# One fused block on one core: the first keys by two queues, and the masks of some attention groups added by VectorE

## The chip, the cores and the metric

The kernel runs on one core of a Trainium2 chip. The metric is the device time of one execution in microseconds, the median of three runs. Engines are named as in the profile: PE is TensorE, DVE is VectorE, ACT is ScalarE, POOL is GpSimd, SP is SyncE. ACTq and SPq are the queues through which ScalarE and SyncE issue transfers (DMA).

## What is computed

Four batches of 576 tokens pass through three parts in a row: masked attention with 8 heads of 64, a gated feed-forward part with a product over the tokens, and a part with a sine and a cosine of projected phases and two more products over the tokens.

```python
scores = scale * np.matmul(q, k.transpose(0, 1, 3, 2))
mask_local = (rel >= 0) & (rel < 32)
mask_strided = (rel >= 0) & (pos[None, :] % 32 == pos[:, None] % 32)
scores = np.where(masks, scores, -1e9)            # heads 0-3 local, 4-7 strided
attn = softmax(scores); x = attn @ v              # heads side by side: 512 columns
h = np.maximum(x @ w_in, 0.0); u, v = halves of h
v_s = einsum('ts,bsd->btd', w_spatial, normalised v) + b_spatial
x = (u * v_s) @ w_out
theta = x @ w_theta; zr, zi = x * cos(theta), x * sin(theta)
y = w_tok_r applied to zr + w_tok_i applied to zi (over the tokens)
u = x + y; out = u + np.maximum(u @ w_ch, 0.0)
```

## The kernel before, in words

All matrix weights and activations are split into a high and a low float16 part, and each product is made of three TensorE products (`PASS`). The stages of a batch, by the names of the PSUM tiles, are `v`, then `u` and `sp` (the gated part), `x` (`w_out`), `th` (the phases), `y` (the tokens) and `c` (the last product). The loop at the end of the kernel runs them batch after batch, and the `v` products of the next batch stand ahead of the `y` products of this one.

The phase stage makes one tile `th` for each of four column blocks (`z_chunk`, line 953). ScalarE copies it to whole turns in a tile `ta`, VectorE subtracts these from the phase in PSUM (the first VectorE step on `ta`, which lets go of the PSUM tile), ScalarE takes the sines, VectorE multiplies by `x2f`, and high and low parts go to `vn` and by transposing transfers to `zf`. There are three such PSUM tiles (`pm`, line 202), shared by all stages; a fourth product tile waits until one of them is read out.

Weights come as raw 64-bit words. ScalarE, VectorE and GpSimd turn them into high and low parts while the first batch runs (`stage` and `from_f64`, lines 226 and 233; `tok_part`, line 306). `raw` tiles are the buffers `x2f`, `zf` and `xT`; the 32-bit value is `wx`; `win`, `wtok` and so on are the finished parts. GpSimd makes most low parts.

Attention of batches 0 to 2 is in float32, by nine groups of blocks (`groups`, line 423): groups 0 to 3 are four local blocks of 96 columns of keys each for head pair 0 or 1, group 4 the two last local blocks, groups 5 to 8 strided blocks of 64 columns. So a group is 384 columns wide, but group 4 has 192 and group 8 has 256. Group 6 also holds two blocks at the end of the sequence that are only 36 columns wide.

For each group `gr_scores` (line 504) makes the scores in PSUM and adds the mask there by one more TensorE product, or two, with the identity in bfloat16 (`identb`) and the mask repeated over the blocks. `gr_shift` (line 533) has VectorE take the row maxima from PSUM and write the scores minus maximum to `sm`. Then come the exponential (`gr_exp`), the transposes to `pT` (`gr_turn`), the product with the values and the division (`gr_pv`), and the transposes to `xT` (`gr_out`).

`attention0` (line 606) is batch 0. Nothing else runs beside it, and its instructions stay in program order on each engine. At its start SyncE loads query and keys of head pair 0 for the first four blocks, then ScalarE's queue loads the whole of pair 1, and a small exponential makes ScalarE load its table. `load_qk` (line 429) issues one transfer for the queries and two for the two heads' keys. Before it, `WARM` dummy products of the identity with itself run on TensorE (line 1077). `attention1` (line 661) makes batches 1 and 2 beside the stages of the batch before, a step at a time, each step due at a time in the table `ATT_AT`. Outside `attention0` a scheduler settles the order on each engine, with priority for the stages over attention. Batch 3 goes another way (`attention`, line 747), whose mask comes by a transfer and a cast on GpSimd (`load_mask16`, line 499). GpSimd casts it ahead of the low parts of `win`.

Of the kernel before, what the change touches and what calls it, by code (L numbers as in the profile page):

```python
# [17 lines left out]
AF = mybir.ActivationFunctionType  # L18
ALU = mybir.AluOpType
# [31 lines left out]
E_YLO = 'gggggggg'  # L51
E_YHI = 'vaavvaav'
E_ZLO = 'vvvvvvvv'
WARM = 6
ATT_AT = (None, (2.7, 3.9), (79.0, 5.4), (169.9, 4.6))
CONV_SP = (20.0, 9.9, 1.9)
CONV_OUT = (37.0, 12.0, 5.0)
# [8 lines left out]
def kernel(  # L66
# [52 lines left out]
    nc = Engines  # L119
    B, DM, S = out.shape  # L120
    P = 128
# [40 lines left out]
    halfpi = const.tile([P, 1], F32, name="halfpi")  # L162
# [30 lines left out]
    x2f = const.tile([P, NC, S], F32, name="x2f")  # L193
# [228 lines left out]
    QB, CB = 64, 54  # L422
# [3 lines left out]
               (False, [(3, i) for i in range(6)]), (False, [(3, i) for i in range(6, 10)])]  # L426
    NG = len(groups)

    def load_qk(b, hp, q, k, c0, c1, by=None):
        by = by or nc.sync  # L430
        local = hp < 2
        src = kzl[b, hp] if local else kzs[b, hp - 2]
        k0, k1 = (c0 + STRIDE if c0 else 0, c1 + STRIDE) if local else (c0, c1)
        by.dma_start(q[:, c0:c1], qp[b, hp][:, c0:c1])
        for j in range(2):
            h = slice(64 * j, 64 * j + 64)
            by.dma_start(k[h, k0:k1], src[h, j, k0:k1])

    def load_vl(b, hp, v):
        src = vl_d[b, hp].rearrange("p n j d -> p n (j d)")  # L440
# [60 lines left out]
        nc.sync.dma_start(mf, mask_d)  # L501
        nc.gpsimd.tensor_copy(mask, mf)

    def gr_scores(g, q, k, sc):

        local, blocks = groups[g]
        w = 96 if local else QB
        n = len(blocks)
        if local and blocks[0][1] == 0:
            runs = [(0, 1, mask64[:, 1]), (1, n, mask64[:, 0])]  # L510
        else:
            runs = [(0, n, mask64[:, 0] if local else mask54)]
        first = groups[g][0]

        def masks():
            for r0, r1, m in runs:
                nc.tensor.matmul(sc[:, r0 * w:r1 * w].rearrange("p (n c) -> p n c", c=w), identb,
                                 m.unsqueeze(1).broadcast_to([P, r1 - r0, w]), start=(not first and r0 == 0),
                                 stop=(first and r1 == n))

        if not first:
            masks()
        for i, (hp, blk) in enumerate(blocks):
            o = (QB if local else CB) * blk
            m, c = min(QB, S - o), w if local else min(w, S - o)
            for j in range(2):
                h = slice(64 * j, 64 * j + 64)
                nc.tensor.matmul(sc[64 * j:64 * j + m, i * w:i * w + c], q[hp][h, o:o + m], k[hp][h, o:o + c],
                                 start=(first and i == 0), stop=(not first and i == n - 1))
        if first:  # L530
            masks()

    def gr_shift(g, sc, sm, st):
        local, blocks = groups[g]
        n, w = len(blocks), 96 if local else QB
        mx = st[:, 0, 0:n]
        sv = sc[:, 0:n * w].rearrange("p (n c) -> p n c", c=w)
        nc.vector.tensor_reduce(out=mx, in_=sv, op=ALU.max, axis=mybir.AxisListType.X)
        nc.vector.tensor_tensor(sm[:, 0:n * w].rearrange("p (n c) -> p n c", c=w), sv,
                                mx.unsqueeze(2).broadcast_to([P, n, w]), ALU.subtract)  # L540
# [65 lines left out]
    def attention0(aside):  # L606
# [6 lines left out]
        q, k = [t[:, 0] for t in qk], [t[:, 1] for t in qk]  # L613
        v = [vf[:, i * 9 * VW:(i + 1) * 9 * VW].rearrange("p (n d) -> p n d", n=9) for i in range(2)]
        v23 = vf[:, 18 * VW:30 * VW].rearrange("p (h n d) -> p h n d", h=2, n=6)
        v += [v23[:, i] for i in range(2)]
        load_qk(0, 0, q[0], k[0], 0, 4 * QB)
        load_qk(0, 1, q[1], k[1], 0, S, nc.scalar)
        nc.scalar.activation(x2f[:, 0, 0:1], halfpi, AF.Exp)
        make_masks()  # L620
        load_qk(0, 0, q[0], k[0], 4 * QB, S)
        load_vl(0, 0, v[0])
# [8 lines left out]
        for s in range(NG + 3):  # L631
            mid, end = aside.get(s, ((), ()))
            if s < NG:
# [6 lines left out]
                sm, pT = t[:, 0, 0:384], t[:, 1, 0:512].rearrange("p (n k) -> p n k", n=4)  # L640
                st = att_p.tile([P, 2, 6], F32, tag="st", name="st", bufs=4)
# [3 lines left out]
            if s >= 3:  # L645
                banks, sm, pT, st = un.pop(s - 3)
# [14 lines left out]
    def attention1(b):  # L661
        q, k, v = {}, {}, {}
# [19 lines left out]
        for s in range(NG + 3):  # L682
            if s < NG:
                sm = att_p.tile([P, 384], F32, tag="sm", name="sm", bufs=2)
                pT = att_p.tile([P, 4, P], F32, tag="pT", name="pT32", bufs=2)
                st = att_p.tile([P, 2, 6], F32, tag="st", name="st", bufs=4)
                un[s] = (sm, pT, st)
            if s >= 3:
                gr_out(b, s - 3, xs.pop(s - 3), pa("sc"))
            if 2 <= s < NG + 2:  # L690
                sm, pT, st = un.pop(s - 2)
                pv = pa("av")[:, 0:3 * VW].rearrange("p (i n) -> p i n", i=3)
                gr_pv(s - 2, v, pT, pv, st, pT)
                xs[s - 2] = pT
            if s < NG:
                sm, pT, st = un[s]
                sc = pa("sc")
                gr_scores(s, q, k, sc)
                gr_shift(s, sc, sm, st)
                gr_exp(s, sm)  # L700
            if s in loads:
                f, hp = loads[s]
                f(hp)
                if s == 4:
                    load_a(3)
            if 1 <= s <= NG:
                sm, pT, st = un[s - 1]
                gr_turn(s - 1, sm, pa4("av"), pT)
            yield
# [485 lines left out]
```

## Time and profile before

| | |
|---|---|
| median of 3 runs | 505.43 us (505.38, 505.43, 506.62) |
| the profiled execution | 506.96 us, its span 505.1 us |
| TensorE busy | 485.1 us of the span |
| VectorE, ScalarE, GpSimd busy | 284.8, 267.8, 92.9 us |
| granted TensorE clock, mean over the span | 0.996 |
| transfers | 52.72 MB, mean 104 GB/s |

Times within the span are counted from its start. Busy time of an engine is the time in which it works on an instruction. In the timeline a row is one instruction, or a run of like ones with their count, with the start and the time it took; what stands in brackets is the idle time of the engine before it and what ended that. The operands are written as output, arrow, inputs, with the names of the tiles. All operations are recorded by one helper, so all have the line L103.

### The profile page before, as it was taken

The numbers are of one execution on the slowest core, as the hardware profiler recorded it, in microseconds if no ns is written. First come the engines' busy times: TensorE is split into PE (matmuls) and PEld (weight loads), VectorE is DVE, ScalarE is ACT, GpSimd is POOL, SyncE is SP. The second block draws the span as 40 slices with busy tenths as digits, with TensorE's granted clock in tenths as the row PEclk, the third lists the DMA queues.
The fourth block names the chain that finished last, engine by engine and source line by source line (L and its number), as shares of the span: only waits on it lengthen the run. The fifth ranks groups of instructions, "written<-read, shape, count | busy, mean of one in ns | idle before, by whom it ended". The sixth has DMA issues, their size and how long they took to land. (4 is left out here: it accounts for less than half of the span.)

```text
span 505.1 us, 10834 instructions
## 1 busy us (share of the span) xinstructions
PE 485.1 (96%) x4460; PEld 364.4 (72%) x4460; DVE 284.8 (56%) x607; ACT 267.8 (53%) x475; POOL 92.9 (18%) x91
## 2 busy tenths in 40 slices
PE   7889989998999999999999989999999999999996
PEld 5655757776567777888758867777657777777774
DVE  3765986555699343473499578772587121227412
ACT  2657788587994233345672757754862022149202
POOL 2042147225124400021003210021005200210220
PEclk9999999999899999999999999999999999999999
DMA  6868748377691024221080156230160020003402
GB/s 177 279 203 234 260 151 270 103 185 225 188 223 49 1 66 150 72 80 27 1 185 4 31 128 195 47 60 5 38 151 1 1 95 1 0 2 80 111 1 93
DMA packets 71788, 52.72 MB, mean 104 GB/s; under 512 B 50552, under 2 KB 59960, under 8 KB 71738
## 3 DMA queue, kind: packets, MB, share of 16 engines
q1 hardware_dynamic: 71434, 51.42, 36.5%
q8 instruction: 35, 0.57, 0.5%
q10 hardware_dynamic: 304, 0.61, 0.4%
q14 instruction: 15, 0.12, 0.1%
HBM read 35.36 MB, written 4.72 MB: 79 GB/s over the span
## 5 line engine op out<-in xcount | busy, mean ns | idle before, releaser
L103 PE MATMUL y<-wtok,zf 128*128 128x288 f16 x864 | 107.2, 286 | 1.0 <-DMA zf<-vn 1.0
L103 PEld LDWEIGHTS <-zf 128*128 128x128 f16 x864 | 84.1, 98 | 23.5 <-DMA zf<-vn 1.3
L103 PE MATMUL sp<-wsp,vn 128*128 128x288 f16 x384 | 52.2, 286 | 1.6 <-ACT vn L103 1.3
L103 PE MATMUL c<-x2h,wch 128*128 128x288 f16 x384 | 49.3, 286 | 2.3 <-ACT o L103 2.3
L103 PE MATMUL th<-x2h,wth 128*128 128x288 f16 x384 | 49.6, 291 | 2.0 <-DVE ta L103 2.0
L103 PE MATMUL x<-zf,wout 128*128 128x288 f16 x384 | 49.9, 286 | 0.0
L103 PE MATMUL u<-xT,win 128*128 128x288 f16 x384 | 49.7, 286 | 0.0
L103 PE MATMUL v<-win,xT 128*128 128x512 f16 (+1 forms) x240 | 48.4, 380 | 0.8 <-DVE xT L103 0.6
L103 PEld LDWEIGHTS <-vn 128*128 128x128 f16 x416 | 39.7, 98 | 12.1 <-ACT vn L103 1.4
L103 POOL TENSOR_TENSOR x2h<-x2f,x2h 128x576 f16<-128x576 f32 x20 | 25.5, 1279 | 119.1 <-ACT x2h L103 47.2
L103 PEld LDWEIGHTS <-wth 128*128 128x128 f16 x384 | 38.1, 100 | 12.5 <-issue 2.2
L103 PEld LDWEIGHTS <-wch 128*128 128x128 f16 x384 | 37.3, 98 | 11.8 <-issue 2.7
L103 PEld LDWEIGHTS <-win 128*128 128x128 f16 x384 | 37.3, 98 | 9.2
L103 PEld LDWEIGHTS <-wout 128*128 128x128 f16 x384 | 36.7, 98 | 9.6
L103 PEld LDWEIGHTS <-xT 128*128 128x128 f16 (+1 forms) x240 | 21.0, 100 | 25.2 <-issue 2.2
L103 ACT ACTIVATE x2h<-x2f 128x576 f16<-128x576 f32 (+1 forms) x28 | 20.9, 746 | 28.9 <-DVE x2f L103 28.4
L103 DVE SCALAR_TENSOR_TENSOR x2f<-y,x2f 128x576 f32<-128x576 f32 x16 | 12.0, 753 | 30.6 <-PE y L103 30.5
L103 DVE TENSOR_TENSOR u<-u,sp 128x576 f32<-128x576 f32 x16 | 12.0, 752 | 28.2 <-PE sp L103 28.2
L103 ACT ACTIVATE o<-c 128x576 f32<-128x576 f32 (+1 forms) x17 | 10.4, 616 | 32.1 <-PE c L103 31.8
L103 DVE TENSOR_TENSOR ta<-ta,x2f 128x1152 f32<-128x1152 f32 x16 | 21.5, 1354 | 9.8 <-ACT ta L103 9.8
L103 POOL TENSOR_TENSOR zf<-u,zf 128x576 f16<-128x576 f32 x8 | 10.7, 1340 | 86.0 <-ACT zf L103 86.0
L103 DVE TENSOR_TENSOR vn<-ta,vn 128x1152 f16<-128x1152 f32 x16 | 21.5, 1355 | 5.6 <-ACT vn L103 5.6
(140 smaller groups left out, 738.2 us busy)
## 6 DMA issues: line engine op xcount, KB each, us to landing
out_dram<-o SPq DMA_DIRECT2D x15, 288.0 KB
kt<-in_qp_dram SPq DMA_DIRECT2D x8, 288.0 KB
qs<-in_qd_dram SPq DMA_DIRECT2D x8, 288.0 KB
x2f<-in_w_in_dram SPq DMA_DIRECT2D x2, 1024.0 KB
zf<-in_w_in_dram SPq DMA_DIRECT2D x2, 1024.0 KB
xT<-in_w_ch_dram SPq DMA_DIRECT2D x2, 1024.0 KB
kt<-in_kzl_dram SPq DMA_DIRECT2D x8, 152.0 KB
ks<-in_kl_dram SPq DMA_DIRECT2D x4, 304.0 KB
```

Source lines behind the costliest of these rows:

```text
L103: ins = f(*args, **kwargs)
```

## The change

`WARM` is 7 in place of 6. `load_qk` takes a second queue for the second head's keys; the first load of all uses SyncE and ScalarE. The small exponential, and with it the table load, now stands ahead of ScalarE's three transfers of pair 1. `gr_scores` can leave the mask out and then hands it on; `gr_shift` then adds it on VectorE while it copies the scores to `sm`, and takes maximum and difference from there. `attention1` does so for batch 2, and for batch 1 from group 4 on, but never for group 6.

```diff
@@
-WARM = 6
+WARM = 7
@@
-    def load_qk(b, hp, q, k, c0, c1, by=None):
+    def load_qk(b, hp, q, k, c0, c1, by=None, by1=None):
@@
         for j in range(2):
             h = slice(64 * j, 64 * j + 64)
-            by.dma_start(k[h, k0:k1], src[h, j, k0:k1])
+            ((by1 if j else None) or by).dma_start(k[h, k0:k1], src[h, j, k0:k1])
@@
-    def gr_scores(g, q, k, sc):
+    def gr_scores(g, q, k, sc, add=True):
@@
-        if not first:
+        if not add:
+            first = True
+        elif not first:
             masks()
@@
                 nc.tensor.matmul(sc[64 * j:64 * j + m, i * w:i * w + c], q[hp][h, o:o + m], k[hp][h, o:o + c],
-                                 start=(first and i == 0), stop=(not first and i == n - 1))
-        if first:
+                                 start=(first and i == 0), stop=(not (first and add) and i == n - 1))
+        if first and add:
             masks()
-
-    def gr_shift(g, sc, sm, st):
+        return [] if add else runs
+
+    def gr_shift(g, sc, sm, st, runs=()):
+
@@
         sv = sc[:, 0:n * w].rearrange("p (n c) -> p n c", c=w)
+        for r0, r1, m in runs:
+            to = sm[:, r0 * w:r1 * w].rearrange("p (n c) -> p n c", c=w)
+            nc.vector.tensor_tensor(to, sv[:, r0:r1], m.unsqueeze(1).broadcast_to([P, r1 - r0, w]), ALU.add)
+        if runs:
+            sv = sm[:, 0:n * w].rearrange("p (n c) -> p n c", c=w)
         nc.vector.tensor_reduce(out=mx, in_=sv, op=ALU.max, axis=mybir.AxisListType.X)
@@
-        load_qk(0, 0, q[0], k[0], 0, 4 * QB)
+        load_qk(0, 0, q[0], k[0], 0, 4 * QB, None, nc.scalar)
+        nc.scalar.activation(x2f[:, 0, 0:1], halfpi, AF.Exp)
         load_qk(0, 1, q[1], k[1], 0, S, nc.scalar)
-        nc.scalar.activation(x2f[:, 0, 0:1], halfpi, AF.Exp)
@@
-                gr_scores(s, q, k, sc)
-                gr_shift(s, sc, sm, st)
+                gr_shift(s, sc, sm, st, gr_scores(s, q, k, sc, b == 1 and s < 4 or s == 6))
```

The scheduler's order on the engines moves with it. On ScalarE, at the start of the program (`kt_80` is head pair 0's tile, `kt_81` pair 1's; minus before, plus the change):

```order
+L103 DMA kt_80<-in_kzl_dram 64x288
+L103 ACT_TABLE_LOAD
+L103 ACTIVATE x2f<-halfpi 128x1
 L103 DMA kt_81<-in_qp_dram 128x576
 L103 DMA kt_81<-in_kzl_dram 64x608 x2
-L103 ACT_TABLE_LOAD
-L103 ACTIVATE x2f<-halfpi 128x1
```

One key transfer came to this queue, and pair 1's three moved behind the table load.

On ScalarE, in the phase stage of batch 0 (`xT_94` holds the last raw weight), before:

```order
L103 ACTIVATE xT_94<-xT_94 128x576
L103 ACTIVATE wtok<-wx 128x1152
L103 ACTIVATE wx<-xT_94 128x576
L103 ACTIVATE ta_1549<-th_1493 128x576
L103 ACTIVATE ta_1566<-th_1494 128x576
L103 ACTIVATE ta_1602<-th_1577 128x576
L103 ACTIVATE ta_1549<-ta_1549 128x576
L103 ACTIVATE wtok<-wx 128x576
L103 ACT_TABLE_LOAD
```

and now:

```order
L103 ACTIVATE xT_94<-xT_94 128x576
L103 ACTIVATE wx<-xT_94 128x576
L103 ACTIVATE ta_1550<-th_1494 128x576
L103 ACTIVATE ta_1567<-th_1495 128x576
L103 ACTIVATE wtok<-wx 128x1152
L103 ACTIVATE ta_1550<-ta_1550 128x576
L103 ACTIVATE ta_1567<-ta_1567 128x576
L103 ACT_TABLE_LOAD
```

The `wtok` write of 1152 columns went behind the first two phase copies, and the third phase copy went behind the table load and the first sines.

On VectorE at the same place, before:

```order
L103 SCALAR_TENSOR_TENSOR ta_1549<-th_1493,ta_1549 128x576
L103 SCALAR_TENSOR_TENSOR ta_1566<-th_1494,ta_1566 128x576
L103 SCALAR_TENSOR_TENSOR ta_1602<-th_1577,ta_1602 128x576
L103 TENSOR_REDUCE st<-sc 128x4
L103 TENSOR_TENSOR sm<-sc,st 128x384
L103 TENSOR_TENSOR ta_1549<-ta_1549,x2f 128x1152
L103 TENSOR_TENSOR vn<-ta_1549,vn 128x1152
L103 TENSOR_TENSOR ta_1566<-ta_1566,x2f 128x1152
L103 TENSOR_TENSOR ta_1602<-ta_1602,x2f 128x1152
L103 SCALAR_TENSOR_TENSOR ta_1638<-th_1613,ta_1638 128x576
```

and now:

```order
L103 SCALAR_TENSOR_TENSOR ta_1550<-th_1494,ta_1550 128x576
L103 SCALAR_TENSOR_TENSOR ta_1567<-th_1495,ta_1567 128x576
L103 TENSOR_TENSOR sm<-sc,mask_100 128x96
L103 TENSOR_TENSOR sm<-sc,mask_100 128x288
L103 TENSOR_REDUCE st<-sm 128x4
L103 TENSOR_TENSOR sm<-sm,st 128x384
L103 TENSOR_TENSOR ta_1550<-ta_1550,x2f 128x1152
L103 TENSOR_TENSOR ta_1567<-ta_1567,x2f 128x1152
L103 SCALAR_TENSOR_TENSOR ta_1603<-th_1578,ta_1603 128x576
L103 TENSOR_TENSOR vn<-ta_1550,vn 128x1152
L103 TENSOR_TENSOR vn<-ta_1567,vn 128x1152
L103 TENSOR_TENSOR ta_1603<-ta_1603,x2f 128x1152
```

The two mask additions of batch 2's group 0 came in, and the third step on `ta` moved behind two multiplications by `x2f`; the fourth stands directly behind the last row shown.

## Rows read from the trace of the kernel before

**Rows 1.** The page's part 1: busy time, share of the span, instructions

```profile
PE 485.1 (96%) x4460; PEld 364.4 (72%) x4460; DVE 284.8 (56%) x607; ACT 267.8 (53%) x475; POOL 92.9 (18%) x91
```

**Rows 2.** Waits of TensorE by releaser: total us, times, longest us

```profile
PE th L103 <- DVE ta L103: 2.0, 1, 2.0
```

**Rows 3.** Timeline of the start: start us, us, engine, operation [idle before <-releaser]

```profile
1.18 1.19 ACTq L103 DMA_DIRECT2D kt<-in_kzl_dram  x2
1.20 1.44 SPq L103 DMA_DIRECT2D kt<-in_kzl_dram  x2
...
1.36 2.93 PE L103 MATMUL av<-ident 128*128 128x128 f32 x12 [1.36 <-POOL ident masks.py:199]
...
5.04 5.30 SPq L103 DMA_DIRECT2D wtok<-in_vl_dram  x8
...
6.00 2.13 PE L103 MATMUL at<-kt 64*64 64x96 f32 x16 [1.71 <-DMA kt<-in_kzl_dram]
...
8.49 1.54 PE L103 MATMUL at<-kt 64*64 64x96 f32 x16
...
14.22 0.88 PE L103 MATMUL sc<-kt 64*64 64x96 f32 x16
```

**Rows 4.** Timeline from 26 us: mask transfer, GpSimd, first v products

```profile
27.25 0.36 SPq L103 DMA_DIRECT2D mf<-in_mask_dram  x1
...
30.81 0.85 POOL L103 CAST mask<-mf 128x512 bf16<-128x512 f32 x1 [26.68 <-DMA mf<-in_mask_dram]
...
31.62 2.26 POOL L103 TENSOR_TENSOR win<-x2h,win 128x512 f16<-128x512 f32 x2
...
33.94 0.38 PE L103 MATMUL v<-win,xT 128*128 128x512 f16 x1 [0.27 <-POOL win L103]
```

**Rows 5.** Timeline from 112 us: the phase stage of batch 0

```profile
121.25 0.73 ACT L103 ACTIVATE xT<-xT 128x576 f32<-128x576 f32 x1 [1.65 <-DMA xT<-in_w_ti_dram]
121.89 1.16 ACT L103 ACTIVATE wtok<-wx 128x1152 f16<-128x1152 f32 x1
...
122.94 0.72 ACT L103 ACTIVATE wx<-xT 128x576 int32<-128x576 uint8 x1
...
123.69 1.32 DVE L103 SCALAR_TENSOR_TENSOR wx<-xT,wx 128x576 int32<-128x576 int32 x1 [2.60 <-ACT wx L103]
124.94 1.41 DVE L103 SCALAR_TENSOR_TENSOR ta<-th,ta 128x576 f32<-128x576 f32 x2
...
125.73 4.66 PE L103 MATMUL th<-x2h,wth 128*128 128x288 f16 x24 [2.02 <-DVE ta L103]
...
130.22 11.94 PE L103 MATMUL v<-win,xT 128*128 128x512 f16 x60
...
137.35 0.75 DVE L103 SCALAR_TENSOR_TENSOR ta<-th,ta 128x576 f32<-128x576 f32 x1
```

**Rows 6.** Timeline of TensorE from 230 us: all phase products of batch 1

```profile
238.34 11.92 PE L103 MATMUL th<-x2h,wth 128*128 128x288 f16 x96
```

**Rows 7.** Windows: stretch, busy us (instructions) by engine, granted clock, DMA share, GB/s

```profile
7.00:8.00 1.00, 1.00 (x14) 0.83 (x10) 0.00 (x0) 0.00 (x0) 0.00 (x0) 1.00 0.63 161
16.00:17.00 1.00, 0.91 (x20) 0.66 (x19) 1.00 (x3) 0.95 (x3) 0.00 (x0) 1.00 1.12 323
127.00:128.00 1.00, 1.00 (x6) 0.62 (x5) 1.00 (x2) 0.98 (x3) 0.00 (x0) 0.50 0.98 401
```

**Rows 8.** Timeline from 145 us: one mask product and the product behind it

```profile
162.85 0.34 PE L103 MATMUL sc<-mask,identb 128*128 128x384 bf16 x1
...
163.03 0.60 PE L103 MATMUL av<-ident,sm 128*96 128x128 f32 x4
```

**Rows 9.** Timeline from 145 us: VectorE beside GpSimd, and alone

```profile
155.17 2.27 POOL L103 TENSOR_TENSOR wch<-wx,wch 128x512 f16<-128x512 f32 x2 [2.25 <-ACT wch L103]
...
156.38 1.28 DVE L103 TENSOR_TENSOR rs<-rs 128x5 f32<-128x5 f32 x2
...
157.89 0.37 DVE L103 TENSOR_TENSOR rs<-rs 128x5 f32<-128x5 f32 x2
```

## The prediction

> **What bounds the kernel now.** I read the page's busy times first: TensorE is busy for 96% of the span [rows 1]. The time is TensorE's own work plus its waits, and an edit counts only if it shortens one of the two. The list of waits by releaser came next: one wait of 2.0 us for a VectorE product on `ta` stands out [rows 2]. Then I read the timeline at the start, at about 30 us and at about 122 us, and the windows for the clock and the transfers.
>
> *Start.* The six dummy products run from 1.36 for 2.93 us, to 4.29; the first scores start at 6.00, after 1.71 us of waiting for a key transfer. SyncE issues the two key halves one after the other (1.44 us) while ScalarE's queue sends the second pair. 16 score passes take 1.54 us at 8.49, but 0.88 at 14.22: the same work, first at little more than half the speed [rows 3].
>
> *At 34 us.* A v product waits 0.27 us for GpSimd's low parts of `win`. GpSimd had stood behind the cast of batch 3's mask, and that behind its transfer, which SyncE issues at 27.25, behind its other first loads: cast at 30.81, low parts from 31.62 to 33.88 [rows 4]. However early the scores are done, this point moves only as far as SyncE's queue moves.
>
> *Phase stage.* From 121 to 126 us one chain sets the end. ScalarE converts the last raw weight when it lands (121.25), writes a `wtok` part (1.16 us), starts the next (0.72), and only then copies the phases; VectorE needs 1.32 us for `wx` and half of 1.41 for the first `ta`, and at 125.73 TensorE has a PSUM tile again [rows 5]. Behind that wait the granted clock is 0.50, the 1.2 GHz level, of 2.4 [rows 7]. The 24 phase products last from 125.73 to the v products at 130.22, 4.49 us [rows 5]. In batch 1, 96 of them take 11.92, so 24 take 2.98 [rows 6]. The low clock costs 1.5 us there, beside the wait.
>
> **The change part by part.** The profiled execution took 506.96 us, its span 505.1. The median of the runs shown is 505.43, 1.5 less.
>
> *A, first loads.* One key half, 0.72 us (half of 1.44), leaves SyncE's queue, and the second pair goes behind ScalarE's table load. All that SyncE issues later can come 0.72 sooner. The ends are 1.3 (if the second half's issue was also slowed as much again by the other queue's, 1.19 us at the same time [rows 3]) and 0: at 16 us the transfer engines are full (1.12), and a queue that is early there may only wait for bytes. At 7 us they are at 0.63 [rows 7] and can make up the delayed second pair; so I take 0.7, nearest the issue row. The first scores themselves may gain more, up to 1.2 us, but that ends in the wait at 34 us. The second pair is needed only by the third group; the scores of two groups (2.13 and 1.54 us [rows 3]) stand ahead of it.
>
> The Trainium skill, "DMA: Bandwidth & Descriptors", section Rules for kernel authors, speaks against this part: halves of the partitions sent by two queues share the same engines, and only the issue time is saved. By that rule A is 0.72, and the first scores gain no more either.
>
> *The dummy.* 2.93 us for six is 0.49 each [rows 3]. Seven end at 4.78, before 6.00, so the key's transfer hides it. If the keys land by 4.3, it costs 0.49 there, and the wait at 34 us hides that.
>
> *B, masks of batch 1's groups 4, 5, 7 and 8.* A 384-column mask product holds TensorE from its start to the next one's: 162.85 to 163.03, 0.18 us [rows 8]. 192 columns by proportion 0.09, 256 columns 0.12. Sum 0.09 + 2 x 0.18 + 0.12 = 0.57, taken as 0.6. The ends are 0, if TensorE then waits behind them, and the row's own length, 0.34 each, 1.4.
>
> *C, phase stage.* ScalarE's `wtok` write now stands behind two phase copies instead of ahead of them. The `wx` step is ready 1.16 us sooner, and the wait of 2.02 shrinks to 0.9 or less. With that I expect the clock to stay up, which returns the 1.5: 2.7 together. Against it, the fourth `ta` step now has one more long VectorE step ahead of it. Before, it ended at 138.10 (137.35 + 0.75). The v products that need its tile are the last 12 of 60, a fifth of 11.94 us, so from 139.8 [rows 5]: 1.7 us of slack. TensorE, 2.7 sooner, meets it and loses 1.0. C is 1.7. The ends are 0 (the wait only moves to `ta` steps three and four) and 2.7. Batch 2's group 0 has its masks inside the old wait: nothing.
>
> *D, masks of batch 2's groups 1 to 5, 7 and 8.* Five of 384 columns (groups 1, 2, 3, 5, 7), one of 192, one of 256: 5 x 0.18 + 0.09 + 0.12 = 1.11, in stretches where TensorE has no wait; I take 1.1. The ends are 0 and 2.4, as for B. The cover is VectorE: each group costs it one more pass, some 0.56 us by today's passes over the same 384 columns, 12 groups about 6 us. It is busy 56% of the span [rows 1], and the exponentials are needed a step later; if that cover goes, TensorE's next wait is for `sm`.
>
> Sum: 0.7 + 0.6 + 1.7 + 1.1 = 4.1, so 506.96 - 4.1 = 502.9 for a run like the profiled one. Two of the three runs lie at 505.4, 1.5 below it: the size of the clock's loss in the phase stage. My reading (an estimate) is that the clock stayed up in those. For them C is 1.7 - 1.5 = 0.2 and the sum 2.6: 505.43 - 2.6 = 502.8. Both ways lead to the same place; I take **502.8 us**.
>
> **Rivals.**
> 1. *All of it comes off the median.* If the 1.5 between profiled run and median is not the clock's, C counts whole: 505.43 - 4.1 = 501.3. For it: nothing shows the clock of the unprofiled runs. Against it: one of them took 506.62 too. 0.15.
> 2. *The phase stage gives nothing, the queue half.* The v products wait for the late `ta` steps as long as the phase products did, and A is 0.4: 505.43 - 0.4 - 1.7 = 503.3. For it: ScalarE's table load and sines now come ahead of the third phase copy. 0.18.
> 3. *The masks were free.* If TensorE waits for VectorE's sums instead, B, C and D vanish and half of A remains: 505.0. For it: VectorE is close behind the scores at each group. Against it: what needs the result stands a step later. 0.13.
> 4. *Slower: VectorE blocked by GpSimd.* Today's subtraction reads PSUM; the new one reads two tiles in SBUF. What that can cost shows where VectorE did it beside GpSimd's `wch` parts: two small `rs` products took 1.28 us, alone 0.37 [rows 9], 0.9 lost. With the added pass, a group is later by 0.9 + 0.56 = 1.5. It decides from the point where that exceeds the slack of its step. If it does in half of the 12 groups, TensorE waits up to 6 x 1.5 = 9.0: 505.43 + 9.0 - 4.1 = 510.3. Against it: GpSimd is busy 18% of the span [rows 1]. 0.05. The Trainium skill, "SBUF — State Buffer", section Who interferes with whom, has it as a rule: a VectorE instruction with two SBUF inputs and a GpSimd instruction that reads SBUF exclude each other for the whole instruction. The trace agrees at the row named.
> 5. *Full speed sooner at the start.* From 6.00 to the fast passes TensorE runs at about half speed. If the longer dummies end that at the first scores, the stretch up to the fast pass at 14.22, at most 8.2 us [rows 3], takes half, 4.1 less. The wait at 34 us takes all of it beyond A: 502.8 again, or, if that wait gave way by as much, 502.8 - (4.1 - 0.7) = 499.4. 0.03. The Trainium skill, "TensorE: Matmul & The Clock Gate", Part 1, says that activity lifts the clock; by it the gain would be there.
>
> **How the numbers follow.** Chances: forecast 0.46; rivals 0.15, 0.18, 0.13, 0.05, 0.03. A measurement of this kernel can tell about 0.3%, 1.5 us, from no change. Faster by more are the forecast and rivals 1, 2 and 5: 0.82. Within it is rival 3: 0.13. Slower is rival 4: 0.05. The range, 500.5 to 504.3, takes in rival 1 with A at 1.3 (500.7) and rival 2 with half of B and D gone (504.2), and leaves rivals 3 and 4 out, 0.18.
>
> **What would show it.** Right, step by step: first scores at 4.8 to 5.5 us; the mask transfer issued at about 26.5 and the v product behind GpSimd's parts at about 33.2; less than 1 us of waiting ahead of the last 24 phase products of batch 0, and a granted clock of 1.0 behind it; y products from about 139.1 (142.16 less 0.7, 0.6 and 1.7); 19 mask products in place of 33; the timeline from batch 3 on as before, only sooner. Wrong: new TensorE waits for `sm` or `pT` on VectorE; v products of batch 1 that wait over 1 us for `ta`; or the v product at 34 us no sooner than before.

## The result: 1.1% slower

The change costs time. Over six runs of each the kernel after takes 1.0108 times the kernel before, 95% interval 1.0060 to 1.0156: medians 510.75 us (508.11 to 514.62) against 505.74 (504.56 to 507.02). The forecast was 502.8, with a range of 500.5 to 504.3. The profiled execution is the slowest of the six, 514.62 us with a span of 512.8, so some of its waits are larger than a middling run's. In all ratios below, runs more than 1.5% above the fastest of their kernel are left out.

The page's part 1 of the kernel after answers to [rows 1]:

```profile
PE 482.6 (94%) x4448; PEld 362.8 (71%) x4448; DVE 297.1 (58%) x621; ACT 267.8 (52%) x475; POOL 97.3 (19%) x91
```

The masks did leave TensorE: it is busy 2.5 us less. But the span is 7.7 longer, so it now waits 30.2 us (512.8 - 482.6) where it waited 20.0. Its waits by releaser in the kernel after (total us, times, longest):

```profile
PE at L103 <- DVE xT L103: 6.4, 2, 5.3
PE sc L103 <- DMA kt<-in_kzs_dram: 2.5, 1, 2.5
...
PE av L103 <- ACT pT L103: 1.4, 2, 0.7
...
PE th L103 <- DVE ta L103: 1.3, 1, 1.3
...
PE av L103 <- DVE pT L103: 1.1, 2, 0.6
```

The wait that the forecast watched, `th` for `ta`, fell from 2.0 [rows 2] to 1.3. Others are new. The start of the kernel after (timeline; start us, us, engine, operation, idle before):

```profile
4.01 6.68 SPq L103 DMA_DIRECT2D wtok<-in_vl_dram  x8
5.27 0.95 PE L103 MATMUL at<-kt 64*64 64x96 f32 x16 [0.56 <-DMA kt<-in_kzl_dram]
...
7.61 1.02 PE L103 MATMUL at<-kt 64*64 64x96 f32 x16 [1.12 <-DMA kt<-in_kzl_dram]
...
10.79 0.55 SPq L103 DMA_DIRECT2D x2f<-in_w_in_dram  x1
...
11.89 3.27 SPq L103 DMA_DIRECT2D xT<-in_kzs_dram  x2
...
19.47 1.10 ACT L103 ACTIVATE x2f<-x2f 128x1024 f32<-128x1024 f32 x1 [4.55 <-DMA x2f<-in_w_in_dram]
...
22.37 0.48 PE L103 MATMUL at<-mask,identb 128*128 128x384 bf16 x1 [5.35 <-DVE xT L103]
...
29.69 0.36 SPq L103 DMA_DIRECT2D mf<-in_mask_dram  x1
```

The first scores come as forecast, at 5.27, and fast: 16 passes in 0.95 us, where they took 2.13 before and 0.88 at 14.22 [rows 3]. What follows does not. The second group's keys (row 7.61) keep TensorE waiting 1.12 us. The value loads begin at 4.01 instead of 5.04 [rows 3] but take 6.68 us to issue instead of 5.30, so SyncE issues the first quarter of `w_in` at 10.79, no sooner than before (10.44). The two loads from 11.89 then take 3.27 us to issue, 1.14 before, and the mask goes out at 29.69, 2.4 later than [rows 4]. ScalarE stands 4.55 us before that quarter's cast with its PSUM copies behind it; VectorE's `xT` needs these, and TensorE, which needs the tile, stands 5.35 us. Other traces with a changed start, taken further down, have a shorter wait at this place: 2.03 us in E3, 1.21 in E15, 0.73 in E2. Windows of the kernel after (us, busy by engine, granted clock, DMA share, GB/s):

```profile
20.00:24.00 4.00, 1.63 (x23) 1.23 (x24) 2.04 (x5) 2.58 (x5) 0.00 (x0) 0.50 0.89 284
84.00:90.00 6.00, 3.50 (x28) 2.18 (x26) 1.98 (x2) 3.73 (x5) 3.37 (x3) 0.78 0.99 268
```

Behind the wait of 5.35 the granted clock is 0.50, the 1.2 GHz level. Behind the wait for keys (2.5 us, second row of the list of waits) its mean is 0.78.

### The profile page after: what moved, and what is told of

Read it like the earlier page. It is cut to its first block, busy times and chain, and to the rows that moved or that the text cites. A ratio compares the mean times of both kernels' runs of the same rounds, so it can differ in the third digit from the quotient of the medians.

```text
span 512.8 us, 10820 instructions
## 1 busy us (share of the span) xinstructions
PE 482.6 (94%) x4448; PEld 362.8 (71%) x4448; DVE 297.1 (58%) x621; ACT 267.8 (52%) x475; POOL 97.3 (19%) x91
## 5 line engine op out<-in xcount | busy, mean ns | idle before, releaser
L103 POOL TENSOR_TENSOR x2h<-x2f,x2h 128x576 f16<-128x576 f32 x20 | 27.6, 1382 | 119.2 <-ACT x2h L103 48.4
L103 PE MATMUL th<-x2h,wth 128*128 128x288 f16 x384 | 48.0, 286 | 1.3 <-DVE ta L103 1.3
L103 ACT ACTIVATE x2h<-x2f 128x576 f16<-128x576 f32 (+1 forms) x28 | 20.9, 745 | 31.6 <-DVE x2f L103 31.2
```

What stands on the lines that cost most here:

```text
L103: ins = f(*args, **kwargs)
```

## The experiments

Ratios are to the kernel before, run beside it on the same chip, with 95% intervals. A per mille is half a microsecond. There is no E8. No kernel with an edit that does nothing was run, so it is not known how far the times of two kernels lie apart for that alone; differences of two or three per mille between kernels are to be read with care.

| | kernel | ratio |
|---|---|---|
| E1 | masks part alone | 1.0038 [1.0013, 1.0062] |
| E2 | start part alone | 1.0074 [1.0034, 1.0113] |
| E3 | after, second pair ahead of the table load | 1.0083 [1.0053, 1.0113] |
| E4 | after, keys not split | 1.0021 [0.9991, 1.0050] |
| E5 | before, once more | one run, 504.48 us |
| E6 | masks of batch 1 alone | 1.0034 [1.0010, 1.0057] |
| E7 | masks of batch 2 alone | 1.0013 [0.9987, 1.0039] |
| E9 | after, cast of `w_in` one group later | 1.0102 [1.0053, 1.0151] |
| E10 | split alone | 1.0044 [1.0013, 1.0074] |
| E11 | late second pair, seven dummies | 1.0077 [1.0041, 1.0113] |
| E12 | split, second pair's queries first | 1.0043 [1.0014, 1.0071] |
| E13 | start part with six dummies | 1.0049 [1.0018, 1.0081] |
| E14 | seventh dummy alone | 1.0059 [1.0033, 1.0085] |
| E15 | after with six dummies | 1.0050 [1.0030, 1.0070] |
| E16 | late second pair alone | 1.0085 [1.0057, 1.0113] |
| E17 | masks of batch 1's groups 4, 7, 8 | 1.0061 [1.0034, 1.0087] |
| E18 | masks of batch 1's groups 5, 7, 8 | 1.0023 [1.0003, 1.0044] |
| E19 | groups 4, 7, 8 and batch 2 | 1.0040 [1.0018, 1.0061] |

Seven of the seventeen ratios fell outside all the ranges set out for them: E2, E4, E6, E10, E11, E16 and E17 (E6, E10 and E16 by less than a per mille).

**The two halves (E1, E2).** From the kernel after, E1 puts the start back, E2 the masks:

```diff
-        load_qk(0, 0, q[0], k[0], 0, 4 * QB, None, nc.scalar)
-        nc.scalar.activation(x2f[:, 0, 0:1], halfpi, AF.Exp)
+        load_qk(0, 0, q[0], k[0], 0, 4 * QB)
         load_qk(0, 1, q[1], k[1], 0, S, nc.scalar)
+        nc.scalar.activation(x2f[:, 0, 0:1], halfpi, AF.Exp)
```
```diff
-                gr_shift(s, sc, sm, st, gr_scores(s, q, k, sc, b == 1 and s < 4 or s == 6))
+                gr_shift(s, sc, sm, st, gr_scores(s, q, k, sc, True))
```

E1 has `WARM = 6` too. Expected of E1 and E2:

> The masks part alone: batch 2's seven groups and batch 1's last four by VectorE, the start as in the kernel before. Theory (the start alone makes the loss, the masks gain as the prediction summed them, 0.6 + 1.1, with up to 1.7 in the phase stage): 1.7 to 3.4 us under the kernel before, a ratio of 0.993 to 0.997, and no wait of over 1 us at 20 us. Rival 1 (the masks cost nothing on TensorE and VectorE's extra adds lengthen a chain): ratio 1.003 to 1.011, most of the change's loss. Rival 2 (the masks were free): ratio 0.999 to 1.001.

> The start part alone (keys split over two queues, second pair behind the table load, seven dummies), all masks on TensorE. Theory: the loss is here, ScalarE waits some 4.5 us for the first quarter of w_in at about 19 us and TensorE some 5 us behind it; ratio 1.010 to 1.018 (the changed kernel's 1.0108 and the masks' gain on top). Rival 1 (the masks are the loss): ratio 0.998 to 1.001. Rival 2 (masks free): 1.009 to 1.012.

Each half loses: the masks 1.9 us, the start 3.7. Together that is 5.6, near the whole change's 5.5, with intervals of 1.2 us either way for the masks and 2.0 for the start. For the masks rival 1 holds. For the start my theory was wrong too: 1.0074 lies under its range, and E2 has no long wait for `w_in`. TensorE's timeline in E2, and its window behind the second row:

```profile
19.78 0.32 PE L103 MATMUL at<-mask,identb 128*128 128x384 bf16 x1 [0.73 <-DVE xT L103]
...
83.71 0.29 PE L103 MATMUL sc<-kt 64*64 64x64 f32 x2 [2.17 <-DMA kt<-in_kzs_dram]
```
```profile
84.00:88.00 4.00, 4.00 (x36) 2.84 (x36) 2.34 (x3) 1.77 (x4) 3.24 (x3) 0.57 0.56 215
```

Laid against E5, the kernel before in the next paragraph, E2 is level up to the products of `sp` (first one at 64.61 us, E5 64.74) and 3.6 us behind at those of `x` (96.02, E5 92.40). Between the two stand a wait of 2.17 us for batch 1's strided keys and a granted clock of 0.57 behind it, where E5 has 1.00. Why the keys land late stays open.

**The kernel before once more (E5).** All ratios need a trace of the kernel before whose clock stays up. Expected:

> The kernel before itself, one more profiled execution, as the thing to lay the others' traces against. Theory (the kernel before varies from run to run, 503.6 to 510.0 us in the runs so far, by two or three waits for late data and the clock that falls after them): where this run's clock is 0.998 or more, its span is 502 to 503.5 us, the products of the fourth transformed stretch in batch 1 start without a lower clock, and v of batch 1 starts at some 128.5 instead of 130.2 us [the phase stage loses its 1.5 us]. Rival: its times agree with the first profile within 0.3 us everywhere.

It took 504.48 us, with a span of 502.7. TensorE's timeline in E5:

```profile
6.25 1.95 PE L103 MATMUL at<-kt 64*64 64x96 f32 x16 [1.97 <-DMA kt<-in_kzl_dram]
...
32.30 1.24 PE L103 MATMUL v<-win,xT 128*128 128x512 f16 x5 [0.56 <-DVE xT L103]
...
125.25 3.10 PE L103 MATMUL th<-x2h,wth 128*128 128x288 f16 x24 [1.71 <-DVE ta L103]
128.19 2.11 PE L103 MATMUL v<-win,xT 128*128 128x512 f16 x9
```

and its window behind the wait at 125:

```profile
126.00:130.00 4.00, 4.00 (x29) 2.61 (x27) 1.78 (x3) 3.97 (x6) 1.27 (x1) 1.00 1.00 326
```

The wait is there (1.71 us), yet the clock stays at full speed and the 24 products take 3.10 us, where [rows 5] had 4.66. So the 1.5 us that step C wanted back is lost in some runs of the kernel before and not in others. Nor does the length of the wait decide it. E10 below waits longer at this place and keeps its clock. Its timeline and window:

```profile
125.61 3.10 PE L103 MATMUL th<-x2h,wth 128*128 128x288 f16 x24 [2.20 <-DVE ta L103]
```
```profile
126.00:130.00 4.00, 4.00 (x30) 2.72 (x28) 2.00 (x4) 3.91 (x6) 1.30 (x2) 1.00 0.92 315
```

Where a start is compared with one trace below, it is E5's.

**The start, part by part (E3, E4, E10, E16, E14, E11, E13).** E3 and E4 undo one edit each in the kernel after:

```diff
# E3
-        nc.scalar.activation(x2f[:, 0, 0:1], halfpi, AF.Exp)
         load_qk(0, 1, q[1], k[1], 0, S, nc.scalar)
+        nc.scalar.activation(x2f[:, 0, 0:1], halfpi, AF.Exp)
# E4
-        load_qk(0, 0, q[0], k[0], 0, 4 * QB, None, nc.scalar)
+        load_qk(0, 0, q[0], k[0], 0, 4 * QB)
```

E10, E16 and E14 make one edit each in the kernel before; E11 is E16 and E14 together, E13 is E10 and E16 together:

```diff
# E10
-        load_qk(0, 0, q[0], k[0], 0, 4 * QB)
+        load_qk(0, 0, q[0], k[0], 0, 4 * QB, None, nc.scalar)
# E16
+        nc.scalar.activation(x2f[:, 0, 0:1], halfpi, AF.Exp)
         load_qk(0, 1, q[1], k[1], 0, S, nc.scalar)
-        nc.scalar.activation(x2f[:, 0, 0:1], halfpi, AF.Exp)
# E14
-WARM = 6
+WARM = 7
```

Expected, first of the pair that undoes one edit, then of the edits alone:

> The changed kernel, but with the second pair's three transfers issued ahead of the table load again; the first keys stay split over two queues. Theory A (the second pair's transfers started too late and share the engines with the value loads, so that the first quarter of w_in lands late): the wait at 19 us is gone, ratio to the kernel before 0.993 to 0.998. Theory B (the split itself lets SyncE's queue run ahead by half a microsecond, and its value loads take the place of the second pair's keys): the wait stays, ratio 1.008 to 1.013.

> The changed kernel, but with both first key halves on SyncE's queue again; the second pair's transfers stay behind the table load. Theory A (second pair late): the wait at 19 us stays, ratio 1.005 to 1.013, since the first scores lose their 0.7 us besides. Theory B (the split): ratio 0.993 to 0.998.

> The split of the first keys over two queues alone: second pair's transfers ahead of the table load, six dummies, all masks on TensorE. Theory (the split is what the start loses by; the table load's place and the dummy do nothing): as the start-only kernel, ratio 1.005 to 1.010. Rival (the loss needs the split together with the table load's place): 0.998 to 1.003.

> Second pair's transfers behind the table load and seven dummies, both key halves on SyncE's queue, all masks on TensorE: the start without the split. Theory (neither costs anything; the masks cost 1.9 us of the 1.05 us that the table-first kernel lost, so that this is slightly faster): ratio 0.996 to 1.000. Rival (these two are neutral and the table-first kernel's 1.05 us against the masks-only kernel's 1.9 us was spread): 0.999 to 1.003.

> The start part without the seventh dummy: split, second pair behind the table load, six dummies, masks on TensorE. Theory (the dummy is nothing; the split and the late second pair add up): ratio 1.005 to 1.009, as the start-only kernel with seven. Rival (the seventh dummy costs, since all four traces with the split and seven dummies show batch 1's strided keys 1.1 to 2.5 us late at 83 to 87 us, and the split alone with six does not): 1.003 to 1.005, and no wait for these keys.

> The kernel before with seven dummies instead of six and nothing else. Theory D (the seventh dummy makes batch 1's strided keys late: they are 1.1 to 3.3 us late in five of the six traces with seven dummies and in none of the eight with six): a wait of over 1 us for these keys at 82 to 86 us, ratio 1.003 to 1.008. Theory S (the dummy is nothing and that pattern is chance): no wait or a rare one, ratio 0.998 to 1.002.

> The kernel before with the second pair's transfers behind the table load and nothing else: six dummies, both key halves on SyncE's queue, all masks on TensorE. Theory D (the 3.9 us of the kernel with this and seven dummies are the dummy's): ratio 0.998 to 1.002. Theory S (they come from the second pair's late start): 1.004 to 1.008.

E3 spoke for the split as the cause, and so did E4 in part (it fell between its two ranges). The edits alone then contradicted it: 2.2 us for the split, 3.0 for the dummy, 4.3 for the late second pair, and not more for two or three together (E11 3.9, E13 2.5, E2 3.7). The losses do not add, and no single edit was found to be the cause. E16 shows best where the gain of an early start goes. TensorE's timeline in E16:

```profile
4.46 0.55 PE L103 MATMUL at<-kt 64*64 64x96 f32 x2 [0.17 <-DMA kt<-in_kzl_dram]
6.04 1.54 PE L103 MATMUL at<-kt 64*64 64x96 f32 x14 [1.03 <-DMA kt<-in_kzl_dram]
...
31.89 1.24 PE L103 MATMUL v<-win,xT 128*128 128x512 f16 x5 [0.56 <-DVE xT L103]
...
38.44 1.25 PE L103 MATMUL sc<-kt 64*64 64x96 f32 x16 [1.82 <-DMA kt<-in_kzl_dram]
```

Its window behind the last row:

```profile
40.00:44.00 4.00, 4.00 (x26) 1.89 (x25) 2.28 (x6) 2.81 (x4) 0.00 (x0) 0.57 1.08 334
```

The first two score passes come 1.8 us before E5's, but the next fourteen wait 1.03 us, and all sixteen are done at 7.58, 0.6 before E5's 8.20. By the first `v` product 0.4 is left (31.89 for 32.30). Batch 1's keys then take 1.82 us and the clock falls to 0.57; at the first `u` products E16 is 3.2 behind (53.42 for 50.23). In all the traces with a changed start the first `v` product stands between 31.2 and 35.4, and in those with the old start between 31.3 and 33.3. The split alone (E10) shows what SyncE's queue does with its saved time. The queue in E5, and then in E10:

```profile
4.94 5.66 SPq L103 DMA_DIRECT2D wtok<-in_vl_dram  x8
10.70 0.55 SPq L103 DMA_DIRECT2D x2f<-in_w_in_dram  x1
```
```profile
4.01 6.61 SPq L103 DMA_DIRECT2D wtok<-in_vl_dram  x8
10.73 0.55 SPq L103 DMA_DIRECT2D x2f<-in_w_in_dram  x1
```

The value loads begin 0.9 us sooner, and the first quarter of `w_in` goes out at the same time. SyncE's waits from 3 to 11 us, in E5 and then in E10 (us, times, longest):

```profile
SPq L103 <- DMA kt<-in_qp_dram: 0.5, 1, 0.5
SPq L103 <- DMA kt<-in_kzl_dram: 0.5, 1, 0.5
```
```profile
SPq L103 <- DMA kt<-in_qp_dram: 1.5, 1, 1.5
...
```

The program of the kernel after says what it waits for. On SyncE's queue each load waits for one of eight completion semaphores that go round over both queues:

```
L103 DMA wtok<-in_vl_dram 32x3x128 [waits DMAHW7_49]
L103 DMA wtok<-in_vl_dram 96x3x128 [waits DMAHW0_49]
L103 DMA x2f<-in_w_in_dram 128x2x512 [waits DMAHW1_49,Activation_49]
```

So a load can go out only when the transfer that used its semaphore before has landed. Behind the first value load SyncE waits 0.5 us so in E5 and 1.5 in E10; behind that one wait the loads go out one upon another in both, at about 0.6 us each. The microsecond of issue time that the split saved is spent in this wait. The Trainium skill, "DMA: Bandwidth & Descriptors", section Rules for kernel authors, has it that splitting over queues saves issue time only. The trace agrees (4.01 for 4.94), and shows besides that the issue time saved is taken back here. This explains why nothing was gained, not why single edits lose 2 to 4 us.

What the seventh dummy costs by itself is not settled. E14's first scores wait 1.89 us for their key, as E5's wait 1.97, and its first `v` product stands at 32.5. The execution traced is the fastest of E14's, at 506.00 us, so it can't hold the whole loss of 3.0. It has one more stretch at a lower clock, behind 66 us, where the kernel before has none:

```profile
68.00:72.00 4.00, 4.00 (x34) 2.75 (x32) 2.44 (x2) 3.09 (x4) 1.75 (x2) 0.70 0.19 15
```

E7, E17 and E19, with six dummies, have one there too, so this trace proves nothing.

**Where the start could be mended (E9, E12, E15).** E9 moves the cast behind the fifth group, E12 sends the second pair's queries ahead of the first key's half, E15 is the change with `WARM = 6`:

```diff
-        3: ((), (a0, b0)),
-        4: ((), (c0,)),
+        3: ((), ()),
+        4: ((), (a0, b0, c0)),
```
```diff
+        nc.scalar.dma_start(q[1][:, 0:S], qp[0, 1][:, 0:S])
         load_qk(0, 0, q[0], k[0], 0, 4 * QB, None, nc.scalar)
+        for j in range(2):
+            h = slice(64 * j, 64 * j + 64)
+            nc.scalar.dma_start(k[1][h, 0:S + STRIDE], kzl[0, 1][h, j, 0:S + STRIDE])
-        load_qk(0, 1, q[1], k[1], 0, S, nc.scalar)
         nc.scalar.activation(x2f[:, 0, 0:1], halfpi, AF.Exp)
```

Expected:

> The changed kernel whole, but the cast of the first quarter of w_in (ScalarE's two operations and the first of VectorE's) is put behind the fifth group's scores instead of the fourth's, so that ScalarE does the next turn's evictions ahead of it. Theory A (the loss of the split is ScalarE waiting for a late w_in ahead of work that TensorE needs, 4.5 us in the changed kernel's profile): the wait shrinks below 2 us and TensorE's 5.35 us at 22 us with it; ratio 1.003 to 1.007 to the kernel before, against the changed kernel's 1.0108. Theory B (the transfers as a whole are late, and the next to be waited for is as late): 1.009 to 1.013.

> The split of the first keys alone, but on ScalarE's queue the second pair's queries (295 KB) go ahead of the first key's half, as in the kernel before they go out at 0.74 us. Theory A (the split loses because the second pair's big transfers start 0.6 us later, so that the engines move some 100 GB/s in the first 4 us where they moved 158, and the shortfall is never made up): about 150 GB/s or more in the first 4 us, ratio 0.998 to 1.002 against the split alone's 1.0044. Theory B (it loses because SyncE's queue runs ahead and its value loads then wait longer for their lanes, 6.6 us instead of 5.3): as the split alone, 1.003 to 1.006, with the value loads issuing for over 6 us.

> The changed kernel with six dummies instead of seven. Theory D: no wait for batch 1's strided keys, and the ratio to the kernel before falls from 1.0108 to about 1.005 (split 1.0044 and masks 1.0038, less some overlap, 1.005 to 1.008). Theory S: 1.008 to 1.013, the wait there or not by chance.

E9 is theory B: ScalarE no longer waits for `w_in`, and TensorE stands 2.31 us for `in_vs`, the loads behind it, instead. E2 has no such wait either and loses 3.7 us, so that wait is not what the start loses by. E12 moves 143 GB/s in the first 4 us, near the 156 of E5 (the split alone 86), and its value loads take 5.74 us; neither helps, so a shortfall of bytes in the first 4 us is not the cause. E15's 1.0050 is about half of what the change loses, on another chip and with an interval that touches that of the change; it fits the dummy's own loss, without showing it.

**The masks, part by part (E6, E7, E17, E18, E19).** All have the start of the kernel before and other groups in the last argument of `gr_scores`, which says whose masks TensorE adds:

```diff
-gr_scores(s, q, k, sc, b == 1 and s < 4 or s == 6)
+gr_scores(s, q, k, sc, b == 2 or s < 4 or s == 6)            # E6
+gr_scores(s, q, k, sc, b == 1 or s == 6)                     # E7
+gr_scores(s, q, k, sc, b == 2 or s not in (4, 7, 8))         # E17
+gr_scores(s, q, k, sc, b == 2 or s not in (5, 7, 8))         # E18
+gr_scores(s, q, k, sc, b == 1 and s not in (4, 7, 8) or s == 6)  # E19
```

Expected:

> VectorE adds the masks of batch 1's groups 4, 5, 7 and 8 alone; the start and batch 2 as in the kernel before. Theory (an add on VectorE sits in the chain scores, maximum, exponential, transposes, and delays the product with the values by more than the 0.18 us of TensorE that it saves): four groups of the eleven, so a third to a half of the 1.9 us that all eleven cost, ratio 1.001 to 1.003. Rival (the masks themselves are free or a small gain and the loss of the masks part comes from batch 2 alone, where GpSimd and the imaginary token products run beside): 0.997 to 1.001.

> VectorE adds the masks of batch 2's seven groups alone; all else as in the kernel before. Theory: half to two thirds of the 1.9 us that all eleven cost, ratio 1.001 to 1.004, with the waits of TensorE for ScalarE's and VectorE's halves of the transposed scores that the masks-only kernel shows at 168 and 171 us (0.95 and 0.59 us). Rival (batch 2's masks gain 1.1 us as the prediction had it and the loss comes from batch 1): 0.996 to 0.999.

> The kernel before, with VectorE adding the masks of batch 1's groups 4, 7 and 8 and no others (three of the four): the order of all later work stays as in the kernel before. Theory O (what batch 1's four masks cost is not the adds but the order that the scheduler makes without these products: behind it VectorE's qT operation stands ahead of a softmax maximum of batch 2 near 165 us, and TensorE waits 0.9 us at 169 and 0.7 us at 196): neither wait over 0.3 us, ratio 0.998 to 1.001. Theory A (the adds in the chain cost): 1.002 to 1.004, three quarters of the 1.0034 that all four cost.

> As the kernel with groups 4, 7 and 8, but groups 5, 7 and 8: also three masks, and in this one the order of the stages from 120 to 205 us turns over as with all four. Theory O: both waits are there (0.9 and 0.7 us), ratio 1.002 to 1.005. Theory A: the same as groups 4, 7 and 8, within 0.1%.

> Groups 4, 7 and 8 of batch 1 and batch 2's seven by VectorE, the start as in the kernel before: the masks part of the change but for one group. Theory O: ten of the eleven masks leave TensorE without the turned order, ratio 0.996 to 1.001, 0.3 to 0.8% under the masks-only kernel's 1.0038 with its one more mask. Theory A: 1.002 to 1.004.

In E7 VectorE adds the masks of eight groups of batch 2. The expectation says seven, and E19's says eleven for both batches; group 0 of batch 2, whose gain the prediction put at nothing, makes them eight and twelve. The eight cost nothing that can be told and gain nothing that can be told; batch 1's four cost 1.7 us.

Beside a changed start the masks' loss does not show each time. E15 is E13 with the masks on VectorE, and both are at 1.005; E4 is E11 with them, on another chip, and loses 2.8 us less. So the 1.9 us of E1 is a figure for the old start.

E1 and E5 (both with a mean clock of 0.998) give the balance: TensorE is busy 481.6 against 483.1 us, 1.5 less, and stands 21.4 against 19.6, 1.8 more. These two executions are 0.3 us apart (504.76 and 504.48), E1's being its fastest; so they show where the gain of 1.5 went, and not the rest of the 1.9 that E1 loses over its runs. In E1, by its list of waits from 36 us on, these have grown:

```profile
PE av L103 <- ACT pT L103: 1.6, 2, 1.0
...
PE av L103 <- DVE pT L103: 1.1, 2, 0.6
```

E5 has none of the first and 0.5 of the second. The value product of a group now waits for that group's transposed scores, one step behind the add.

A part comes from elsewhere. E6 has batch 2's masks on TensorE and yet loses 1.0 us in batch 2's attention. E5's timeline there, and then E6's:

```profile
163.99 0.55 DVE L103 TENSOR_REDUCE st<-sc 128x4 f32<-128x384 f32 x1
...
168.14 0.73 PE L103 MATMUL av<-v,pT 96*64 96x65 f32 x16
```
```profile
164.69 2.57 DVE L103 TENSOR_TENSOR qT<-qs,qT 64x576 f16<-64x576 f32 x1
...
167.97 0.55 DVE L103 TENSOR_REDUCE st<-sc 128x4 f32<-128x384 f32 x1
...
169.44 0.74 PE L103 MATMUL av<-v,pT 96*64 96x65 f32 x16 [0.92 <-ACT pT L103]
```

Fewer products in batch 1 make the scheduler order the stages from 120 to 205 us differently; a `qT` step of 2.57 us now stands on VectorE ahead of the group's maximum. I took this for the whole cause, and E17 and E18 say no. E18 has the turned order and loses 1.2 us, E17 keeps the old order and loses 3.1; E19, the old order with eleven of the twelve groups moved, loses 2.0, as much as E1.

In E17 the step of group 4 itself shows. The timeline in E5, with the mask on TensorE, and then in E17:

```profile
75.64 2.85 POOL L103 TENSOR_TENSOR wout<-x2h,wout 128x512 f16<-128x512 f32 x2 [2.30 <-ACT wout L103]
...
77.10 0.36 DVE L103 TENSOR_TENSOR sm<-sc,st 128x192 f32<-128x192 f32 x1
```
```profile
77.03 2.85 POOL L103 TENSOR_TENSOR wout<-x2h,wout 128x512 f16<-128x512 f32 x2 [3.14 <-ACT wout L103]
...
78.11 0.35 DVE L103 TENSOR_TENSOR sm<-sc,mask 128x192 f32<-128x192 f32 x1
...
78.88 1.23 DVE L103 TENSOR_TENSOR sm<-sm,st 128x192 f32<-128x192 f32 x1
...
80.14 0.36 ACT L103 ACTIVATE sm<-sm 128x192 f32<-128x192 f32 x1 [0.57 <-DVE sm L103]
...
81.04 0.73 PE L103 MATMUL av<-v,pT 96*64 96x65 f32 x16 [0.64 <-ACT pT L103]
```

TensorE's wait of 0.64 stands in all traces in which VectorE adds group 4's mask (E1, E3, E4, E6, E9, E15, E17, E19, after) and in none of the others. The add itself takes 0.35. What takes longer is the subtraction behind it: it now reads two tiles in SBUF beside GpSimd's `wout` parts, and takes 1.22 or 1.23 us in all nine traces, where E5's, from PSUM beside the same parts, takes 0.36. Had it taken 0.36 in E17 it would have ended at 79.24 (78.88 + 0.36), and ScalarE, free at 79.57 (80.14 - 0.57), would not have waited; so, by this estimate, the add alone would have fitted. This is rival 4's mechanism at one group. The rest of E17's loss is not accounted for; its trace has two stretches at the lower clock.

## Why the prediction was wrong

The steps are those of the prediction.

**A, first loads, was the largest miss.** The step that failed is "All that SyncE issues later can come 0.72 sooner". It counts issue time only and leaves out that SyncE waits for landings. The value loads did begin about a microsecond sooner, but SyncE then waited for a landing (1.5 us in E10 where E5 waits 0.5), and `w_in` behind them came no sooner: at 10.73 in E10 and 10.79 in the kernel after, where it was 10.44 in the kernel before and 10.70 in E5. The lower end of 0 also failed: it left out a loss without a reason, and the start lost 3.7 us (E2). In E2 that loss falls at batch 1's strided keys, 2.17 us late, and at the low clock behind them; why they are late stays open. The bound at 34 us did not decide either. In the kernel after TensorE waits there for VectorE's `xT` and not for GpSimd, and its first `v` product is at 35.44, where it was at 32.4.

**The dummy** was priced at nothing, hidden by the first key. The key does hide it (E14's scores wait 1.89 us), but E14 loses 3.0 us over its runs, which no step of the prediction has and which stays open.

**B and D, the masks.** The size was right: TensorE's busy time fell by 1.5 us in E1, forecast 1.7. The step that failed is their lower end, "0, if TensorE then waits behind them": the waits are larger than the masks. For B the runs gave a loss of 1.7 us (E6), for D a loss of -0.7 to 2.0 (E7). "What needs the result stands a step later" was the cover, and group 4 shows it gone, by 0.64 us. Its estimate of VectorE's price, "about 6 us", was short too: VectorE is busy 10.6 us more in E1 than in E5 (295.1 for 284.5).

Rival 4's mechanism, at a chance of 0.05, is what undoes the cover at group 4 (1.23 us for 0.36), and it is seen elsewhere: in the kernel after four of the twelve groups have a slowed subtraction (1.22 for 0.36; 0.91, 1.64 and 1.47 for the 0.56 that 384 columns take), in E1 two (1.22 and 1.47). That its 510.3 lies near the measured 510.75 is luck all the same. It supposed six groups at 1.5 us and gains of 4.1 on top, and two thirds of the measured loss are the start's.

**C, phase stage**, had the right place and the wrong sum. In E1, where the clock stays up as in E5, the wait is 1.06 us instead of 1.71, and `v` starts 1.0 sooner (127.22 for 128.19), as does `y`. The prediction had 0.2 for such a run; the loss of 1.0 at the fourth `ta` step did not come. In the kernel after the wait only moves. Its timeline at the same stage:

```profile
125.89 1.25 ACT L103 ACTIVATE zf<-zf 128x1152 f32<-128x1152 f32 x1 [2.44 <-DMA zf<-in_w_ti_dram]
...
129.26 0.33 ACT L103 ACTIVATE xT<-sc 128x216 f16<-128x216 f32 x1
...
130.70 0.37 DVE L103 TENSOR_TENSOR xT<-sc,xT 128x216 f16<-128x216 f32 x1
...
131.12 0.88 PE L103 MATMUL sc<-kt 64*64 64x96 f32 x16 [1.61 <-DVE xT L103]
...
133.25 3.10 PE L103 MATMUL th<-x2h,wth 128*128 128x288 f16 x24 [1.25 <-DVE ta L103]
```

TensorE stands 1.61 + 1.25 = 2.86 us where it stood 2.02. SyncE now issues batch 2's queries ahead of the raw weight `in_w_ti`, which goes out at 118.53, 1.3 us before the first phase product (119.8); before it was 110.57, 2.2 us before (112.8). The prediction followed ScalarE's order and not SyncE's. But E1 has the same order and the same 1.3 us (111.41 and 112.69), and its ScalarE waits 0.42 us for the weight, not 2.44; so the order alone does not explain the wait of the kernel after, which stays open. The clock's part was misread: a wait of 2.02 was followed by 0.50 in the kernel before, one of 2.20 in E10 by 1.00. So the wait alone does not bring the clock down.

**The one estimate across runs**, that the clock had stayed up in the runs at 505.4, agrees with E5. It also means that in such runs C could win only the wait itself, as the prediction's 0.2 has it.

Right were the first scores (5.27, forecast 4.8 to 5.5) and the 19 mask products. The first sixteen passes were fast too, as rival 5 has it, but that the dummies did this is not shown: they are fast in four of the seven traces with seven dummies and in three of the thirteen with six. The granted clock reads 1.00 there in every trace, also where the passes are slow [rows 7], so it can't tell. The Trainium skill, "TensorE: Matmul & The Clock Gate", Part 1, by which activity lifts the clock, had led to rival 5; no run here shows when it rose. Two of the signs that the prediction named for being wrong came: the masks' new waits for `pT`, and a `v` product no sooner than before.

## What to carry to other kernels

Before crediting an edit of a transfer queue with the issue time that it saves, look whether the queue waits for earlier landings further on; then an earlier first transfer buys nothing for those behind that wait. When VectorE takes over a step and then reads two tiles in SBUF, look what GpSimd does at that moment (here 1.23 us instead of 0.36). And give the gain of a moved operation a negative end when it joins a chain that another engine waits for, however idle the engine that takes it.

## What the runs showed beside

- None of the fifteen kernels with only parts of the change came out faster than the kernel before, and single edits of the start cost 2.2 to 4.3 us. The best, E7 and E4, cannot be told from it.
- Batch 1's strided keys are late in five of the seven traces with seven dummies and in none of the thirteen with six: by 1.1 to 2.5 us in E2, E3, E9 and after, by 3.3 in E11, whose traced execution is its slowest. SyncE issues them at the same 76.5 us in E2 as in E5 (76.6). E14 has seven and no such wait, so the dummy alone does not do it; open.
- The transposing transfers ahead of the last batch's `y` products, 450 us behind the edit, keep TensorE waiting 1.0 to 1.1 us in thirteen traces and 1.2 to 2.5 in seven: all those that change the start and leave every mask on TensorE (E2, E10 to E14, E16). I have no cause for it.
- The time varies more than 0.3%: the kernel before took 503.3 to 510.0 us in all but one of its runs beside the experiments (513.95), and the granted clock of the slower ones is mostly lower (1.000 in the one at 503.3, 0.986 in the one at 510.0).
